# The first lane block of a convolution and feed-forward kernel: x copied in parts, the halo and the second block's loads moved back, the lane's first step ahead of conv(2)'s casts

## The chip, the cores and the metric

One NeuronCore of a Trainium2 chip. Its engines run programs of their own and wait for each other through semaphores: TensorE (PE, matmuls), VectorE (DVE), ScalarE (ACT), GpSimd (POOL) and SyncE (SP, which here only issues DMAs). The metric is the device time of one execution in microseconds, the median of several. Shorter is better.

## The reference

`x` has 8 sequences of 4096 tokens of 192 features. A causal convolution over 7 tokens, with one softmax-normalised filter for each of 8 heads of 24 features, is followed by a gated feed-forward layer:

```python
w = softmax(weight)                                  # 8 heads x 7 taps
out = np.einsum('hk,bskhg->bshg', w, x_unf)          # x_unf: the 7 tokens up to s, zeros before the start
x = out.reshape(B * S, D)                            # 32768 x 192
gate = np.maximum(x @ w_gate, 0.0)                   # 192 x 1536
val = x @ w_val
return (gate * val @ w_out).astype(np.float32)       # 1536 x 192
```

Inputs and outputs are float32; the kernel computes in float16 with float32 sums.

## The kernel before

**Units.** The 32768 tokens go through in 16 units of 1024 token positions, for two sequences ("streams") side by side, one stream on partitions 0 to 63 and one on 64 to 127. Line 692 loops over them. A unit is: the hidden layer for its two windows of 512 (`gate_val`, line 569: per group of 128 hidden features a gate and a value matmul, a relu on ScalarE at line 600, a product on VectorE at line 601), then the output projection in six passes (`project_turn`, line 604: three column groups `p`, each once with window 0 first and once with window 1), then VectorE's `turn_out` (line 626), which transposes a finished group into the output tile, and the stores. Between the first and the second pass over a column group ScalarE does a tiny copy out of that group's PSUM (`between_turns`, line 623). PSUM is a ring of four tiles that all of these share, so a late reader holds up TensorE.

**Two ways to convolve.** The tokens of unit 0 and the first window of unit 1 are convolved by TensorE with band matrices: `conv_steps`, and `conv(2)` (line 402) for the third window. `conv(2)` does eight matmuls, five casts from PSUM on ScalarE (line 426) and five transposing DMAs on SyncE (line 445) into `dense[1]`, which unit 1 reads first. All later windows are convolved by "the lane", one block of two windows for each unit, while TensorE works on something else:

- `lane_load(b)`, line 245: GpSimd issues one load of x for each stream (line 254), cast to float16, into `x_e`, which has one buffer. Block 0 alone also loads a "halo", the 16 tokens ahead of it, into `head` (line 264).
- `lane_turn(b)`, line 455: GpSimd copies `x_e` to `x_p` in another order (line 474, one copy for each stream), and SyncE issues eight DMAs that transpose `x_p` into `x_r` (line 477), which has tokens along the free dimension. The halo is copied from the block before (line 460), or, for block 0, is copied out of `head` (line 464) and transposed by a DMA of its own (line 465).
- `lane_first(b)`, line 527: ScalarE multiplies its part of `x_r` by the first tap into `acc` (line 531, two instructions).
- `lane_rest(b)`, line 538: VectorE adds the other taps (line 542) in 13 steps, dealt out between the `turn_out`s.
- `product(b, k)`, line 503: ScalarE makes products for the rest of the columns (line 506, thirteen instructions, dealt out behind the `between_turns`), which GpSimd adds up (`add`, line 513).

**Order.** The program is scheduled by hand: each engine executes its instructions in the order in which the kernel writes them, and waits where an input isn't there or a buffer isn't free. In the start-up GpSimd issues the loads of the weights, of x and of block 0 in a written order, the output weights' load last (line 689, into the tile `prod0`). At unit 0 come `lane_turn(0)`, `lane_load(1)`, two copies that bring the output weights into `Wo` (line 698), the hidden layer, `conv(2)`, and `lane_first(0)`. SyncE's queue holds, from 10 to 52 us, the issues of the taps (line 353), the halo's transpose, the eight of block 0 and the five of `conv(2)`.

Of the kernel before, what the change touches and what calls it, by code (L numbers as in the profile page):

```python
# [9 lines left out]
F16 = mybir.dt.float16  # L10
# [5 lines left out]
def kernel(  # L16
# [12 lines left out]
    nc = tc.nc  # L29
# [7 lines left out]
    NCH = D // 64  # L37
    NBLK = D // 32
    NFF = DFF // 128
    WIN = 512  # L40
# [12 lines left out]
    HALO = 16  # L53
# [3 lines left out]
    TILES = UNIT // 128  # L57
# [6 lines left out]
    epool = ctx.enter_context(tc.tile_pool(name="epool", bufs=1))  # L64
# [99 lines left out]
    with nc.allow_low_precision("one of the terms is not zero"):  # L164
        nc.vector.tensor_reduce(
            out=Z[:, 112 : 112 + HR],
            in_=eye[:].rearrange("p (g i) -> p i g", i=HR),
# [4 lines left out]
        out=mask[:, :, 0],  # L172
# [69 lines left out]
    def windows(b):  # L242
        return [k for k in (2 * b + 3, 2 * b + 4) if k < 2 * NUNIT]

    def lane_load(b, streams=range(2)):


        n = 4 * len(windows(b))
        if b not in xes:
            xes[b] = epool.tile([128, TILES, 2, NCH, 64], F16, name="x_e"), None  # L250
        xe, head = xes[b]
        for st in streams:
            row = NB * st * S + WIN * (2 * b + 3)
            nc.gpsimd.dma_start(  # L254
                out=xe[:, 0:n, st, :, :].rearrange("p j c r -> p j (c r)"),
                in_=bass.AP(
                    tensor=x.tensor,
                    offset=x.offset + row * D,
                    ap=[[D, 128], [128 * D, n], [1, D]],
                ),  # L260
            )
        if 1 in streams and b == 0:
            head = const.tile([HALO, 2, NCH, 64], F16, name="head")
            nc.gpsimd.dma_start(
                out=head[:].rearrange("p s c r -> p s (c r)"),
                in_=bass.AP(
                    tensor=x.tensor,
                    offset=x.offset + (WIN * 3 - HALO) * D,
                    ap=[[D, HALO], [NB * S * D, 2], [1, D]],
                ),  # L270
            )
        xes[b] = xe, head
# [177 lines left out]
    def second_start(b):  # L450


        return HALO + WIN + HALO * (WIN * (2 * b + 4) % S == 0)

    def lane_turn(b):
        xe, head = xes.pop(b)
        xr = rpool.tile([128, NCH, 2 * (HALO + WIN)], F16, name="x_r")
        if head is None:
            end = second_start(b - 1) + WIN
            nc.gpsimd.tensor_copy(out=xr[:, :, 0:HALO], in_=xrs[b - 1][:, :, end - HALO : end])  # L460
        else:
            turned = const.tile([HALO, NCH, 2, 64], F16, name="turned")
            for st in range(2):
                nc.gpsimd.tensor_copy(out=turned[:, :, st, :], in_=head[:, st, :, :])
            nc.sync.dma_start_transpose(
                out=xr[:, :, 0:HALO], in_=turned[:].rearrange("p c s r -> p (c s r)")
            )
        at = second_start(b)
        if at > HALO + WIN:
            nc.gpsimd.memset(xr[:, :, at - HALO : at], 0.0)  # L470
        n = 4 * len(windows(b))
        xp = epool.tile([128, TILES, NCH, 2, 64], F16, name="x_p")
        for st in range(2):
            nc.gpsimd.tensor_copy(out=xp[:, 0:n, :, st, :], in_=xe[:, 0:n, st, :, :])  # L474
        for j in range(n):
            to = HALO + 128 * j if j < 4 else at + 128 * (j - 4)
            nc.sync.dma_start_transpose(  # L477
                out=xr[:, :, to : to + 128],
                in_=xp[:, j].rearrange("p c s r -> p (c s r)"),
            )  # L480
        xrs[b] = xr

# [55 lines left out]
    def lane_rest(b):  # L538
        acc = accs.pop(b)
        for k in range(1, KW):  # L540
            for at, c, t, n in MINE:
                nc.vector.scalar_tensor_tensor(  # L542
                    out=result(b, at, n) if k == KW - 1 else both(acc, b, at, n),
                    in0=shifted(b, c, k, t, n),
                    scalar=tap[:, c, k : k + 1],
                    in1=both(acc, b, at, n),
                    op0=ALU.mult,
                    op1=ALU.add,
                )
                yield  # L550
        at, c, t, n = POOLS[0]
        nc.vector.tensor_scalar(  # L552
            out=both(prods[b, 0], b, at, n),
            in0=shifted(b, c, 0, t, n),
            scalar1=tap[:, c, 0:1],
            scalar2=None,
            op0=ALU.mult,
        )
        yield
# [9 lines left out]
    def gate_val(u, w):  # L569
        h = hpool.tile([128, NFF, 2, WIN], F16, name="hT")  # L570
        xcb, wb = window(u, w)
        for f in range(NFF):
            if u == 0 and w == 0 and f == CONV1:
                for c in range(NCH):
                    ps = psum.tile([128, 2, 512], FP, name="ps")
                    conv_steps(1, ps, c, range(GSUB))
                    evict(nc.scalar.copy, 1, ps, c)
                passed = psum.tile([128, 2, 512], FP, name="ps")
                nc.vector.memset(passed[:, 0, 0:1], 0.0)
            pss = [psum.tile([128, 2, 512], FP, name="ps") for _ in range(2)]  # L580
            order = [(i, c) for i in range(2) for c in range(NCH)]
            if u == 0 and w == 0 and f == 0:
                order.sort(key=lambda ic: ic[1])
            M = 64 if u else 128
            for i, c in order:
                W = (Wg, Wv)[i]
                for q in range(0, 128, M):
                    for st in range(2):
                        nc.tensor.matmul(  # L589
                            out=pss[i][q : q + M, st, :],  # L590
                            lhsT=W[64 * st : 64 * st + 64, c, 128 * f + q : 128 * f + q + M],
                            rhs=xcb[64 * st : 64 * st + 64, wb, c, :],
                            start=(c == 0),
                            stop=(c == NCH - 1),
                            tile_position=(64 * st, q),
                            skip_group_check=True,
                        )
            for sts in [slice(0, 1), slice(1, 2)] if u == 0 and w == 0 and f == 0 else [slice(0, 2)]:
                gr = gpool.tile([128, 2, WIN], F16, name="gr")
                nc.scalar.activation(out=gr[:, sts], in_=pss[0][:, sts], func=ACTF.Relu)  # L600
                nc.vector.tensor_tensor(out=h[:, f, sts], in0=gr[:, sts], in1=pss[1][:, sts], op=ALU.mult)  # L601
        return h
# [89 lines left out]
    for u in range(NUNIT):  # L692
        if u == 0:
            lane_turn(0)
            lane_load(1)
            wide = plain.rearrange("k (f a p d) -> k f a p d", a=2, p=3, d=32)
            for a in range(2):
                nc.gpsimd.tensor_copy(out=Wo[:, :, :, 32 * a : 32 * a + 32], in_=wide[:, :, a, :, :])
        hs = [gate_val(u, w) for w in range(2)]
        if u == 0:  # L700
            dense[1] = xcpool.tile([128, 2, NCH, WIN], F16, name="xc")
            conv(2)
        bp, w0 = u * UNIT // S, u * UNIT % S // WIN
        lane = None
        if u < NBLOCK:
            lane_first(u)
            lane = lane_rest(u)
        o = opool.tile([128, UNIT // 64, D], FP, name="out_s")
        if u == NUNIT - 1:
            for i in range(4):  # L710
                project(bp, w0 + i // 2, hs[i // 2], i % 2, (4, 2, 1, 1)[i], i == 3, o[:, 4 * i : 4 * i + 4, :])
            continue
        tiles = [None] * 3
        for p, turn in ((0, 0), (1, 0), (0, 1), (2, 0), (1, 1), (2, 1)):
            if turn == 0:
                tiles[p] = psum.tile([128, 2, 512], FP, name="ps")
            project_turn(hs, p, tiles[p], turn)
            if turn == 0:
                between_turns(tiles[p])
                if lane:  # L720
                    for k in TAPS[p]:
                        product(u, k)
                continue
            if lane:
                for _ in range(STEPS[p]):
                    next(lane)
            turn_out(tiles[p], o, p)
        store(o, bp, w0)
        if lane:
            add(u, 0)  # L730
        if u + 1 < NBLOCK:
            lane_turn(u + 1)
        if len(windows(u)) > 1:
            add(u, 1)
        if u + 2 < NBLOCK:
            lane_load(u + 2)
# [30 lines left out]
```

## Time and profile before

| | us |
|---|---|
| median of 3 runs | 762.03 (761.94 to 762.22) |
| the profiled execution, whole | 762.57 |
| span of the profiled execution | 760.9 |
| TensorE busy in the span | 756.1 |
| VectorE, ScalarE, GpSimd busy | 675.3, 610.9, 455.2 |

The profile records one execution. Times in its views are microseconds from the start of the span. A row of a time line gives start, duration, engine, line, operation, output and inputs, shape and count, and in square brackets the idle time of the engine ahead of it with what ended it; neighbouring instructions of one kind are merged in one row. "SPq", "POOLq" and the like are the issuing of a DMA or a wait on the engine's own queue. In the DMA views, q0 is the queue of GpSimd's DMAs, q1 that of SyncE's, q8 the fetching of instructions; their columns are packets, megabytes, and the packets' time as a share of 16 DMA engines; the last number of an issue's row is the time from issue to landing. L12 is line 12 of the kernel.

### The profile page before, as it was taken

The page shows a single profiled execution, that of the slowest core. Times are in us where ns is not written, and L with a number is a line of the kernel's source. Part 1 is how long each engine was busy: PE and PEld are TensorE (multiplying, and loading weights), DVE is VectorE, ACT ScalarE, POOL GpSimd, SP SyncE. Part 2 cuts the span into 40 slices and gives each one's busy share as a digit, 9 for nine tenths or more (in the row PEclk, how much of TensorE's full clock was granted, in tenths as well). Part 3 has the DMA queues.
Part 4 walks back from the last instruction along what each step waited for, and adds up shares of the span by engine and source line. Part 5 has one row for each costly group of instructions (what it writes and reads, how often), then busy time and mean ns, then how long its engine had stood idle before and what let it go on. Part 6 is the DMA issues. An engine that isn't in the chain of part 4 may idle for free.

```text
span 760.9 us, 30515 instructions
## 1 busy us (share of the span) xinstructions
PE 756.1 (99%) x13724; PEld 498.7 (66%) x13724; DVE 675.3 (89%) x647; ACT 610.9 (80%) x681; POOL 455.2 (60%) x297
## 2 busy tenths in 40 slices
PE   9999999999999999999999999999999999999998
PEld 5566666666666666666666666666666666666668
DVE  7879989998998989989899899998999989997891
ACT  7888887888888788887887878788797887877671
POOL 8608649195591946929378392874919659193600
PEclk9999999999999999999999999999999999999999
DMA  9944532345323444244444334452244532140402
GB/s 148 155 54 85 85 73 57 44 90 80 85 44 47 102 67 85 50 59 88 62 85 68 58 78 55 85 85 61 63 49 91 79 80 50 23 100 8 85 2 84
DMA packets 154146, 54.23 MB, mean 71 GB/s; under 512 B 149264, under 2 KB 154016, under 8 KB 154016
## 3 DMA queue, kind: packets, MB, share of 16 engines
q1 hardware_dynamic: 117488, 37.83, 24.3%
q0 software_dynamic: 36096, 14.16, 16.5%
q8 instruction: 107, 1.75, 1.0%
q10 hardware_dynamic: 432, 0.30, 0.1%
q14 instruction: 23, 0.19, 0.1%
HBM read 29.21 MB, written 25.17 MB: 71 GB/s over the span
## 4 chain that ended last, share of the span: by engine, by line
PE 92%; POOL 3%; DVE 2%; SPq 1%; DMA 1%; issue 1%; ACT 0%; ACTq 0%; DVEq 0%; POOLq 0%
PE ps L589 61%; PE ps L611 29%; PE ps L654 2%; SPq L477 1%; DVE acc L542 1%; DMA Wv<-in_moe_w_val_dram 1%; DMA x_r<-x_p 1%; POOL Wv L234 0%; DVE out_s L629 0%; POOL x_p L474 0%; POOL Wg L234 0%; POOL out_s L95 0%; POOL Wg L227 0%; POOL x_e L254 0%; POOL Wv L227 0%
## 5 line engine op out<-in xcount | busy, mean ns | idle before, releaser
L601 DVE TENSOR_TENSOR hT<-gr,ps 128x1024 f16<-128x1024 f16 (+1 forms) x385 | 468.7, 1218 | 35.6 <-ACT gr L600 8.4
L600 ACT ACTIVATE gr<-ps 128x1024 f16<-128x1024 f32 (+1 forms) x385 | 393.0, 1022 | 113.4 <-PE ps L589 113.4
L518 POOL TENSOR_TENSOR prod<-prod,prod 128x896 f32<-128x896 f32 x145 | 303.1, 2090 | 260.6 <-DVE prod L552 226.7
L589 PE MATMUL ps<-xc,Wv 64*64 64x512 f16 (+1 forms) x4464 | 324.5, 376 | 0.7 <-DVE out_s L629 0.7
L589 PE MATMUL ps<-xc,Wg 64*64 64x512 f16 (+1 forms) x4464 | 324.4, 376 | 0.0
L611 PE MATMUL ps<-hT,Wo 64*64 64x512 f16 x4320 | 236.1, 376 | 0.0
L589 PEld LDWEIGHTS <-Wg 64*64 64x64 f16 (+1 forms) x4464 | 164.2, 107 | 84.5 <-POOL Wg L234 0.2
L589 PEld LDWEIGHTS <-Wv 64*64 64x64 f16 (+1 forms) x4464 | 157.3, 106 | 92.1 <-issue 1.3
L611 PEld LDWEIGHTS <-Wo 64*64 64x64 f16 x4320 | 155.2, 107 | 77.8 <-issue 0.3
L506 ACT ACTIVATE prod<-x_r,tap 128x1024 f32<-128x1024 f16 (+2 forms) x195 | 182.7, 1018 | 0.0
L542 DVE SCALAR_TENSOR_TENSOR acc<-x_r,tap,acc 128x1024 f32<-128x1024 f16 (+3 forms) x150 | 118.0, 852 | 4.0 <-ACT acc L531 4.0
L629 DVE STREAM_TRANSPOSE out_s<-ps 128x1024 f32<-128x1024 f32 x45 | 56.1, 1247 | 25.8 <-PE ps L611 24.4
L518 POOL TENSOR_TENSOR xc<-prod,prod 128x896 f16<-128x896 f32 x29 | 60.6, 2090 | 2.3
L474 POOL COPY x_p<-x_e 128x1536 f16<-128x1536 f16 (+1 forms) x30 | 42.0, 1430 | 0.0
L254 POOL DMA_DIRECT2D x_e<-in_x_dram x30 | 26.5, 889 | 0.3 <-POOL x_p L474 0.3
L542 DVE SCALAR_TENSOR_TENSOR xc<-x_r,tap,acc 128x1024 f16<-128x1024 f16 (+3 forms) x30 | 25.1, 838 | 0.0
L531 ACT ACTIVATE acc<-x_r,tap 128x1024 f32<-128x1024 f16 (+3 forms) x30 | 22.5, 801 | 1.9 <-DMA x_r<-x_p 1.9
L624 ACT COPY turned_by<-ps 128x2 f32<-128x2 f32 x45 | 6.9, 154 | 16.3 <-PE ps L611 14.5
L654 PEld LDWEIGHTS <-hT 128*128 128x128 f16 x192 | 15.8, 98 | 0.4 <-issue 0.4
L654 PE MATMUL ps<-Wo,hT 128*128 128x192 f16 x192 | 16.0, 246 | 0.0
L665 ACT COPY out_s<-ps 128x768 f32<-128x768 f32 (+2 forms) x5 | 3.2, 640 | 12.7 <-PE ps L654 12.7
L665 DVE COPY out_s<-ps 128x192 f32<-128x192 f32 x1 | 0.4, 356 | 13.3 <-PE ps L654 13.3
(58 smaller groups left out, 68.1 us busy)
## 6 DMA issues: line engine op xcount, KB each, us to landing
out_dram<-out_s SPq DMA_DIRECT2D x123, 192.0 KB
x_e<-in_x_dram POOLq DMA_DIRECT2D x28, 384.0 KB, 6.3
x_r<-x_p SPq DMA_TRANSPOSE x116
prod<-in_moe_w_out_dram POOLq DMA_DIRECT2D x1, 576.0 KB, 8.9
out_s<-in_x_dram POOLq DMA_DIRECT2D x2, 240.0 KB, 6.2
out_dram<-out_s SPq DMA_DIRECT2D x5, 96.0 KB
prod<-in_x_dram SPq DMA_DIRECT2D x2, 192.0 KB
out_s<-in_x_dram POOLq DMA_DIRECT2D x2, 192.0 KB, 6.4
```

Source lines behind the costliest of these rows:

```text
L254: nc.gpsimd.dma_start(out=xe[:, 0:n, st, :, :].rearrange("p j c r -> p j (c r)"), in_=bass.AP(tensor=x.tensor, offset=x.offset + row * D, ...
L474: nc.gpsimd.tensor_copy(out=xp[:, 0:n, :, st, :], in_=xe[:, 0:n, st, :, :])
L506: nc.scalar.activation(out=both(prods[b, k], b, at, n), in_=shifted(b, c, k, t, n), func=ACTF.Copy, scale=tap[:, c, k : k + 1],)
L518: nc.gpsimd.tensor_tensor(out=acc if k < KW - 1 else xcs[b][:, w, :, :].rearrange("p c t -> p (c t)")[:, LDVE : NCH * WIN], in0=acc, in1=p ...
L531: nc.scalar.activation(out=both(accs[b], b, at, n), in_=shifted(b, c, 0, t, n), func=ACTF.Copy, scale=tap[:, c, 0:1],)
L542: nc.vector.scalar_tensor_tensor(out=result(b, at, n) if k == KW - 1 else both(acc, b, at, n), in0=shifted(b, c, k, t, n), scalar=tap[:, c ...
L589: nc.tensor.matmul(out=pss[i][q : q + M, st, :], lhsT=W[64 * st : 64 * st + 64, c, 128 * f + q : 128 * f + q + M], rhs=xcb[64 * st : 64 * ...
L600: nc.scalar.activation(out=gr[:, sts], in_=pss[0][:, sts], func=ACTF.Relu)
L601: nc.vector.tensor_tensor(out=h[:, f, sts], in0=gr[:, sts], in1=pss[1][:, sts], op=ALU.mult)
L611: nc.tensor.matmul(out=ps[64 * st : 64 * st + 64, b, :], lhsT=Wo[64 * r : 64 * r + 64, f, p, :], rhs=hs[b][64 * r : 64 * r + 64, f, st, :] ...
L629: nc.vector.transpose(out=o[:].rearrange("p t (b d) -> p b t d", b=2)[:, :, :, 32 * p : 32 * p + 32], in_=ps[:].rearrange("p b (t c) -> p ...
L654: nc.tensor.matmul(out=ps[:, i // 2, D * (i % 2) : D * (i % 2) + D], lhsT=h[:, f, st, 128 * q : 128 * (q + 1)], rhs=Wo[:, f, :, :].rearran ...
```

## The change

Three things at unit 0, and nothing else:

- In `lane_turn`, block 0's copies to `x_p` are done in halves: for each stream tiles 0 to 3, then tiles 4 to 7, four copies in place of two. The halo's copies and its transposing DMA come behind the block's copies and its eight transposes, on GpSimd and on SyncE. Later blocks have one part, and their halo copy stays ahead.
- `lane_load(1)` is written behind the two copies into `Wo`.
- `conv(2)` is written behind `lane_first(0)`, so that on ScalarE the lane's first step comes ahead of the five casts. The order on TensorE and VectorE is as before.

```diff
         if head is None:
             end = second_start(b - 1) + WIN
             nc.gpsimd.tensor_copy(out=xr[:, :, 0:HALO], in_=xrs[b - 1][:, :, end - HALO : end])
-        else:
+        at = second_start(b)
+        if at > HALO + WIN:
+            nc.gpsimd.memset(xr[:, :, at - HALO : at], 0.0)
+        n = 4 * len(windows(b))
+        xp = epool.tile([128, TILES, NCH, 2, 64], F16, name="x_p")
+        parts = [slice(0, n)] if head is None else [slice(0, n // 2), slice(n // 2, n)]
+        for st in range(2):
+            for js in parts:
+                nc.gpsimd.tensor_copy(out=xp[:, js, :, st, :], in_=xe[:, js, st, :, :])
+        for j in range(n):
+            to = HALO + 128 * j if j < 4 else at + 128 * (j - 4)
+            nc.sync.dma_start_transpose(
+                out=xr[:, :, to : to + 128],
+                in_=xp[:, j].rearrange("p c s r -> p (c s r)"),
+            )
+        if head is not None:
             turned = const.tile([HALO, NCH, 2, 64], F16, name="turned")
             for st in range(2):
                 nc.gpsimd.tensor_copy(out=turned[:, :, st, :], in_=head[:, st, :, :])
             nc.sync.dma_start_transpose(
                 out=xr[:, :, 0:HALO], in_=turned[:].rearrange("p c s r -> p (c s r)")
             )
-        at = second_start(b)
...
-        for st in range(2):
-            nc.gpsimd.tensor_copy(out=xp[:, 0:n, :, st, :], in_=xe[:, 0:n, st, :, :])
...
         if u == 0:
             lane_turn(0)
-            lane_load(1)
             wide = plain.rearrange("k (f a p d) -> k f a p d", a=2, p=3, d=32)
             for a in range(2):
                 nc.gpsimd.tensor_copy(out=Wo[:, :, :, 32 * a : 32 * a + 32], in_=wide[:, :, a, :, :])
+            lane_load(1)
         hs = [gate_val(u, w) for w in range(2)]
         if u == 0:
             dense[1] = xcpool.tile([128, 2, NCH, WIN], F16, name="xc")
-            conv(2)
         bp, w0 = u * UNIT // S, u * UNIT % S // WIN
         lane = None
         if u < NBLOCK:
             lane_first(u)
             lane = lane_rest(u)
+        if u == 0:
+            conv(2)
```

More of the change, by code (lines that the diff above doesn't have):

```diff
@@ L466, in lane_turn @@
                 out=xr[:, :, 0:HALO], in_=turned[:].rearrange("p c s r -> p (c s r)")
-            )
-        at = second_start(b)
[L469 to L472, printed above, removed]
-        for st in range(2):
[L474 to L479, printed above, removed]
             )
```

## The prediction

> **What bounds the kernel now.** I read the page's first lines, then TensorE's waits, then the time lines of TensorE, ScalarE, GpSimd and SyncE between 16 and 62 us, and last the DMA queues stretch by stretch.
>
> ```profile
> span 760.9 us, 30515 instructions
> PE 756.1 (99%) x13724; PEld 498.7 (66%) x13724; DVE 675.3 (89%) x647; ACT 610.9 (80%) x681; POOL 455.2 (60%) x297
> ```
>
> TensorE is busy for 756.1 of 760.9 us. Whatever the change frees on another engine counts only as far as it closes a gap on TensorE, and all gaps together are 4.8 us. Of TensorE's waits for another engine, the only one after the kernel's first 10 us lies where the change works:
>
> ```profile
> PE ps L589 <- DVE out_s L629: 0.7, 1, 0.7
> ```
>
> TensorE's time line shows it:
>
> ```profile
> 41.48 15.80 PE L611 MATMUL ps<-hT,Wo 64*64 64x512 f16 x288
> 57.08 0.84 PE L589 MATMUL ps<-xc,Wg 64*64 64x512 f16 x12
> 57.73 0.85 PE L589 MATMUL ps<-xc,Wv 64*64 64x512 f16 x12
> 58.38 0.84 PE L589 MATMUL ps<-xc,Wg 64*64 64x512 f16 x12
> 59.90 0.84 PE L589 MATMUL ps<-xc,Wv 64*64 64x512 f16 x12 [0.68 <-DVE out_s L629]
> 60.55 0.84 PE L589 MATMUL ps<-xc,Wg 64*64 64x512 f16 x12
> 61.24 0.84 PE L589 MATMUL ps<-xc,Wv 64*64 64x512 f16 x12
> ```
>
> Unit 0's output projection (six passes, 41.48 to 57.08, so 2.60 us each) is followed by unit 1's hidden layer, in groups that start 0.65 us apart (57.73 - 57.08). The sixth group should start at 57.08 + 5 x 0.65 = 60.33 and starts at 61.24. **0.91 us** is lost, and that is all that can be won here. Who loses it is on ScalarE:
>
> ```profile
> 41.14 2.00 ACT L426 CAST out_s<-ps 112x480 f16<-112x480 f32 x5 [0.17 <-PE ps L413]
> 45.08 1.55 ACT L531 ACTIVATE acc<-x_r,tap 128x1024 f32<-128x1024 f16 x2 [1.94 <-DMA x_r<-x_p]
> 46.53 0.14 ACT L624 COPY turned_by<-ps 128x2 f32<-128x2 f32 x1
> ...
> 58.92 1.92 ACT L600 ACTIVATE gr<-ps 128x1024 f16<-128x1024 f32 x2
> ```
>
> ScalarE does conv(2)'s five casts, stands still 1.94 us until the lane's transposed x has landed, does the lane's first step, the little copy of line 624 and thirteen products, and comes to unit 1's first relu at 58.92. VectorE's lane steps hang on the same first step, and its last transpose (58.62) frees the PSUM that the 59.90 group waits for:
>
> ```profile
> 58.62 1.24 DVE L629 STREAM_TRANSPOSE out_s<-ps 128x1024 f32<-128x1024 f32 x1
> ```
>
> So both ways lead back to one moment, the landing of x_r. The chain of waits has it (issue of the last transpose, and the time until it counted as landed):
>
> ```profile
> 40.55 4.21 DMA x_r<-x_p
> ```
>
> I call the moment **T**; it is 44.77 now. The page's execution takes 762.57 us for a span of 760.9; the runs' median is 762.03. I work out differences in the span and put them on the median.
>
> **The change, part by part.** What T costs first. Now the relu starts 13.84 us after the lane's first step (58.92 - 45.08), which starts 0.31 after T. The change puts the casts behind that step: from start to start they take about 1.95 us. The relu then starts at T + 0.31 + 13.84 + 1.95 = T + 16.1. The sixth group starts 2.32 after the relu (61.24 - 58.92), so at T + 18.42, if that is later than 60.33. The loss is T - 41.9 in place of 0.91, and the difference is **T - 42.8**, never under -0.91 (T at 41.9 or before). ScalarE's moved casts are thus no gift: they now fill a hole of 1.94 us, and afterwards they lie behind T. T must come about 2 us earlier for the kernel to stand still.
>
> A second path has the same threshold. The third pass, which adds to the first pass's PSUM, starts at 41.48 + 2 x 2.60 = 46.68 and has to come after the copy of line 624, which reads that PSUM (now done at 46.67). Afterwards that copy ends at T + 0.31 + 1.45 + 1.95 + 0.14 = T + 3.85: in time for T up to 42.8, and from there TensorE waits for it, 1 us for each us of T. Two other users of T have room. VectorE's last transpose ends 15.1 after T and is needed at 59.03, so T up to 43.9. Conv(2)'s transposes:
>
> ```profile
> 26.82 1.22 SPq L465 DMA_TRANSPOSE x_r<-turned  x1
> 29.64 12.17 SPq L477 DMA_TRANSPOSE x_r<-x_p  x8
> 43.16 7.62 SPq L445 DMA_TRANSPOSE xc<-out_s  x5
> ```
>
> ```profile
> 45.69 2.55 SPq L445 DMA_TRANSPOSE xc<-out_s  x2
> ```
>
> ```profile
> 49.36 1.42 SPq L445 DMA_TRANSPOSE xc<-out_s  x1
> ```
>
> The fourth of them is issued at 45.69 + 2.55/2 = 46.97; the fifth overlaps it in the target, waits for its landing and is issued at 49.36. So an undisturbed transpose lands **2.4 us** after its issue starts. The five take 49.36 + 2.4 - 43.16 = 8.6 us from the end of the casts, which will be T + 3.7; TensorE reads the result at 57.08: T up to 44.8.
>
> Now T itself. GpSimd's order around it:
>
> ```profile
> 19.15 0.87 POOL L254 DMA_DIRECT2D x_e<-in_x_dram  x1
> ...
> 23.18 1.03 POOL L689 DMA_DIRECT2D prod<-in_moe_w_out_dram  x1
> 26.17 0.62 POOL L464 COPY turned<-head 16x192 f16<-16x192 f16 x2 [1.96 <-DMA head<-in_x_dram]
> 26.75 2.87 POOL L474 COPY x_p<-x_e 128x1536 f16<-128x1536 f16 x2
> 29.91 1.75 POOL L254 DMA_DIRECT2D x_e<-in_x_dram  x2 [0.30 <-POOL x_p L474]
> 32.16 2.24 POOL L698 COPY Wo<-prod 128x1152 f16<-128x1152 f16 x2 [0.50 <-DMA prod<-in_moe_w_out_dram]
> 59.11 10.75 POOL L518 TENSOR_TENSOR prod<-prod,prod 128x896 f32<-128x896 f32 x5 [24.71 <-ACT prod L506]
> ```
>
> ```profile
> x_e<-in_x_dram POOLq DMA_DIRECT2D x1, 384.0 KB, 6.8
> ```
>
> ```profile
> L474 POOL COPY x_p<-x_e x30: 830/1472/1482, 26.7 to 678.3; 128x1536 f16<-128x1536 f16 x28, 128x768 f16<-128x768 f16 x2
> ```
>
> Today GpSimd stands 1.96 us for the halo rows, copies both streams whole, and the first big transpose starts at 29.64. A half copy (128x768) is 0.83 us in the last lane block. Afterwards the two halves of stream 0 run from 24.21 to 25.9, beside what was a wait; stream 1 lands at 19.15 + 6.8 = 25.95, its first half is copied by 26.8, its second by 27.6, the halo rows by 28.2. Four halves cost 3.3 us for 2.87, hidden, since Wo's copies wait for their DMA until 32.1 anyway. SyncE's tap issues lie ahead of line 465, which started at 26.82, so its queue is free by then. The first transpose can start at **26.8, 2.8 us earlier**. The eight take 12.17 us, the halo's 1.22 now comes behind them: the queue is done at 40.2 (41.8 now). If nothing else held it, the halo's would start at 39.0 and land 2.4 later, T = 41.4: the full 0.91 won.
>
> But something else holds it. The DMA queues between 32.3 and 35 us, in the middle of the 12.17 us in which the eight are issued:
>
> ```profile
> q0 software_dynamic: 1170, 0.44, 143.0%
> q1 hardware_dynamic: 2, 0.00, 0.1%
> ```
>
> q0 is GpSimd's queue (here the second block's two loads), q1 SyncE's. While a load runs, the transposes get 2 packets of 1172. Afterwards Wo's copies go first, 32.16 to 34.40 as now, and the loads are issued at 34.4 to 36.2 in place of 29.9 to 31.7. Nobody waits for them before the next block's copies, which stand behind the sums that begin at 59.11, and Wo's copies, needed at 41.48, lose nothing. The loads move 4.5 us later, from the middle of the transposes to their **end**: the seven earlier ones get through before, the eighth (issued at about 37.7) and the halo's (39.0) meet them. The loads' times to landing, second block's second load of now and the pair of the next block, when no transposes were about:
>
> ```profile
> x_e<-in_x_dram POOLq DMA_DIRECT2D x1, 384.0 KB, 8.0
> ```
>
> ```profile
> x_e<-in_x_dram POOLq DMA_DIRECT2D x2, 384.0 KB, 5.8
> ```
>
> The second load, issued at 35.3, lands between 41.1 (5.8) and 43.3 (8.0). The tail has two transposes to move then; the bounds are nothing and 1 us. T lies between 41.4 and 44.3. I take 42.5 for the load, nearer the 8.0 because two transposes are in its way as seven are now, and 0.5 for the tail: **T = 43.0**, a difference of +0.2.
>
> T itself has an accident in it today. In the stretch from 42 to 44 us (40 slices of 0.05 us):
>
> ```profile
> GB/s 184 210 246 184 225 215 123 67 10 1 1 328 0 0 0 0 0 0 0 0 0 0 0 0 0 0 0 0 0 0 0 0 0 0 0 0 0 0 0 0
> ...
> q8 instruction: 1, 0.02, 3.1%
> ```
>
> The last transpose's data are through at 42.45; then one engine takes a packet of instructions (the 328 at 42.55), and the landing counts at 44.77, 2.3 us after the data, where the fourth transpose above needed 2.4 us for issue, data and all. About 1.6 us of T is that packet (estimate: 2.3 less the 0.7 or so that are left of those 2.4 behind 1.3 of issue and the data). It can miss the new tail or hit it again; I take it as missed, with 0 and +1.6 as bounds.
>
> **A rule of the Trainium skill on this.** "DMA: Bandwidth & Descriptors", section "Queues, rings and completion order", says that each DMA engine goes round between the queues that have work, one packet of some 9 to 17 descriptors at a time. By that the tail would share the engines with the load rather than wait for it, and T would be near 41.4. The 2 packets against 1170 above speak against so fine a turn, so it is a rival and not the forecast.
>
> All later blocks keep one part, and the halo copy stays ahead of it, so nothing changes behind unit 0. GpSimd's next work (59.11) waits for ScalarE's products, and moves with T as TensorE does.
>
> **The rivals.**
> 1. *Full gain.* The tail gets its turn between the loads' packets: T = 39.0 + 2.4 = 41.4, below 41.9, so -0.91: **761.1 us**. For it: SyncE is done 1.6 us earlier even with nine transposes, and the instruction packet may miss. Against: the 1170 to 2.
> 2. *Slower.* The lane's first step stands at the head of ScalarE's queue, and behind it wait the casts, the copy of line 624 and all products, thus TensorE's third pass from 46.68 on. Decides from T = 42.8; at T = 44.3 (second load at 43.3 and the whole 1 us of tail) it costs 1.5, with an instruction packet in the tail (T up to 45) 2.2: **763.2 to 764.2 us**. For it: the q8 row above, and two loads moved onto the tail. Against: the loads get through faster when fewer transposes disturb them (5.8).
> 3. *It doesn't split.* The first transpose waits for all four part copies: start at 27.6, not 26.8, and the halo's at 39.8. As the load ends at 42.5 anyway, T and the time stay as forecast; no case of its own.
>
> **How the numbers follow.** Forecast: T = 43.0, +0.2 us in the span, 762.03 + 0.2 = **762.2 us**, chance 0.58 for T from 42.0 to 44.1 (761.2 to 763.3). Full gain 0.20, slower 0.22. 0.2%, 1.52 us, is about what a measurement of this kernel can tell from no change: faster than 760.5 is not in reach, since the gap is 0.91, so 0.02 for what I overlook; slower than 763.55 needs T above 44.3, half of the second rival, 0.11; the rest, 0.87, is within. The range from 760.9 to 763.8 holds the full gain with 0.2 for the measurement and leaves out the upper part of the second rival, where the tail and the packet both come late.
>
> **What would show it.** Right: the first transpose of the lane at about 26.8 and the last, the halo's, at 38 to 39; the loads' issue at 34.4; between 37 and 41 us q1 with next to no packets beside a full q0; the lane's first step at T + 0.3 with ScalarE idle for 1.5 to 2.5 us before it and the casts right behind it; TensorE's third pass at 46.7 to 47. Wrong: a first transpose that starts at 27.5 or later, or is issued but runs only after 32, when the output weights have landed (they fill q0 until then; if it holds up the whole row and not only the first, T moves out to 44 and the second rival holds); a halo that lands before 42 (the first rival); a sixth group that starts earlier than T + 18.4 after T above 43, which would say that ScalarE's order isn't the binding one.

## The result, and the profile after

The changed kernel takes 764.59 us (median of 14 runs, 763.09 to 765.6), the kernel before 762.21 us on the same chip (14 runs, 761.52 to 763.66). The ratio is 1.0028, 95% interval 1.002 to 1.0036: **slower by 2.1 us**, 1.5 to 2.7 (by the ratio; the medians differ by 2.4), where 762.2 us was forecast with a range up to 763.8. The profiled execution took 764.22 us, with a span of 762.5.

Page and TensorE's waits of the changed kernel:

```profile
span 762.5 us, 30519 instructions
PE 757.0 (99%) x13724; PEld 498.4 (65%) x13724; DVE 675.6 (89%) x647; ACT 610.2 (80%) x681; POOL 455.1 (60%) x299
```

```profile
PE ps L613 <- ACT turned_by L626: 0.9, 1, 0.9
PE ps L196 <- PEq L754: 0.8, 1, 0.8
PE ps L591 <- DVE hT L603: 0.4, 1, 0.4
```

The wait of before is gone (0.7 us for VectorE's transpose), and two others have come in its place: TensorE's third projection pass waits for the little copy out of PSUM, and the sixth group of unit 1 for a product that stands behind a late relu. (The wait at L196 lies in the kernel's first microsecond and is there before as well, with 0.8 us.) Lines behind 460 have moved by two: L613, L626, L591, L602, L508, L533 are the L611, L624, L589, L600, L506, L531 of before. TensorE's time line, with the two gaps in the rows that start at 48.34 and 62.84:

```profile
42.09 5.37 PE L613 MATMUL ps<-hT,Wo 64*64 64x512 f16 x96
48.34 10.55 PE L613 MATMUL ps<-hT,Wo 64*64 64x512 f16 x192 [0.88 <-ACT turned_by L626]
...
62.84 0.84 PE L591 MATMUL ps<-xc,Wv 64*64 64x512 f16 x12 [0.41 <-DVE hT L603]
```

ScalarE, from its last relu of unit 0 on:

```profile
40.55 1.02 ACT L602 ACTIVATE gr<-ps 128x1024 f16<-128x1024 f32 x1 [0.27 <-PE ps L591]
44.80 1.55 ACT L533 ACTIVATE acc<-x_r,tap 128x1024 f32<-128x1024 f16 x2 [3.23 <-DMA x_r<-turned]
46.26 1.97 ACT L426 CAST out_s<-ps 112x480 f16<-112x480 f32 x5
48.10 0.20 ACT L626 COPY turned_by<-ps 128x2 f32<-128x2 f32 x1
```

It stands still for 3.23 us at the lane's first step with the casts ready behind it. The landing T was to come about 2 us earlier to pay for that, and it has hardly moved: 44.49 in place of 44.77. The chain of waits names it, and what follows from it:

```profile
37.96 6.53 DMA x_r<-turned
```

GpSimd and SyncE did what was planned, to a few tenths of a microsecond: four half copies from 24.17, the loads at 34.06, the first transpose at 26.65. The halo's is issued at 37.96, 1 us ahead of the 39.0 of the sum.

```profile
24.17 3.23 POOL L469 COPY x_p<-x_e 128x768 f16<-128x768 f16 x4
27.34 0.63 POOL L479 COPY turned<-head 16x192 f16<-16x192 f16 x2
31.88 2.23 POOL L699 COPY Wo<-prod 128x1152 f16<-128x1152 f16 x2 [3.92 <-DMA prod<-in_moe_w_out_dram]
34.06 1.75 POOL L254 DMA_DIRECT2D x_e<-in_x_dram  x2
```

```profile
26.65 11.21 SPq L472 DMA_TRANSPOSE x_r<-x_p  x8
37.96 1.17 SPq L480 DMA_TRANSPOSE x_r<-turned  x1
```

So the first and the last transpose were issued 3.0 and 2.6 us earlier, and the last landed hardly earlier. The DMA queues from 31 to 33 us, from 37 to 39 and from 39.5 to 42 (packets, megabytes, share):

```profile
q1 hardware_dynamic: 1162, 0.27, 110.3%
q8 instruction: 1, 0.02, 3.7%
q0 software_dynamic: 13, 0.00, 1.7%
```

```profile
q0 software_dynamic: 920, 0.35, 149.2%
q1 hardware_dynamic: 30, 0.00, 2.1%
```

```profile
q0 software_dynamic: 612, 0.23, 111.0%
q1 hardware_dynamic: 455, 0.11, 46.7%
```

First the transposes have the engines to themselves; then the first of the two loads leaves them 30 packets in 950; then the second load and the transposes share, and both are slow. The median of the two loads' times to landing is 7.6 us, and the first alone has 5.9, so the second took 2 x 7.6 - 5.9 = 9.3 us (9.4 unrounded, from 34.93 to 44.3):

```profile
x_e<-in_x_dram POOLq DMA_DIRECT2D x2, 384.0 KB, 7.6
```

```profile
x_e<-in_x_dram POOLq DMA_DIRECT2D x1, 384.0 KB, 5.9
```

### The profile page after: what moved, and what is told of

The parts are those of the page before. It is cut to its first block, busy times and chain, and to the rows that moved or that the text cites. A ratio compares the mean times of both kernels' runs of the same rounds, so it can differ in the third digit from the quotient of the medians.

```text
span 762.5 us, 30519 instructions
## 1 busy us (share of the span) xinstructions
PE 757.0 (99%) x13724; PEld 498.4 (65%) x13724; DVE 675.6 (89%) x647; ACT 610.2 (80%) x681; POOL 455.1 (60%) x299
## 4 chain that ended last, share of the span: by engine, by line
PE 92%; POOL 2%; DMA 2%; ACT 1%; SPq 1%; DVE 1%; issue 0%; ACTq 0%; POOLq 0%
PE ps L591 61%; PE ps L613 29%; PE ps L656 2%; SPq L472 1%; DMA Wv<-in_moe_w_val_dram 1%; DMA x_r<-turned 1%; ACT prod L508 1%; POOL x_p L469 0%; POOL Wg L227 0%; POOL Wv L227 0%; POOL Wv L234 0%; ACT out_s L426 0%; POOL x_e L254 0%; DVE acc L544 0%; ACT acc L533 0%
## 5 line engine op out<-in xcount | busy, mean ns | idle before, releaser
L602 ACT ACTIVATE gr<-ps 128x1024 f16<-128x1024 f32 (+1 forms) x385 | 392.7, 1021 | 113.9 <-PE ps L591 113.8
L591 PE MATMUL ps<-xc,Wv 64*64 64x512 f16 (+1 forms) x4464 | 324.2, 376 | 0.4 <-DVE hT L603 0.4
L591 PE MATMUL ps<-xc,Wg 64*64 64x512 f16 (+1 forms) x4464 | 324.2, 376 | 0.1
L613 PE MATMUL ps<-hT,Wo 64*64 64x512 f16 x4320 | 236.3, 376 | 0.9 <-ACT turned_by L626 0.9
L591 PEld LDWEIGHTS <-Wg 64*64 64x64 f16 (+1 forms) x4464 | 163.6, 107 | 85.2 <-issue 0.4
L591 PEld LDWEIGHTS <-Wv 64*64 64x64 f16 (+1 forms) x4464 | 157.0, 106 | 92.1 <-issue 0.9
L613 PEld LDWEIGHTS <-Wo 64*64 64x64 f16 x4320 | 155.3, 107 | 78.8 <-issue 1.3
L508 ACT ACTIVATE prod<-x_r,tap 128x1024 f32<-128x1024 f16 (+2 forms) x195 | 182.7, 1020 | 0.0
L533 ACT ACTIVATE acc<-x_r,tap 128x1024 f32<-128x1024 f16 (+3 forms) x30 | 22.5, 801 | 3.2 <-DMA x_r<-turned 3.2
L626 ACT COPY turned_by<-ps 128x2 f32<-128x2 f32 x45 | 7.0, 157 | 16.3 <-PE ps L613 14.5
```

The costliest lines, as they stand in the source:

```text
L508: nc.scalar.activation(out=both(prods[b, k], b, at, n), in_=shifted(b, c, k, t, n), func=ACTF.Copy, scale=tap[:, c, k : k + 1],)
L533: nc.scalar.activation(out=both(accs[b], b, at, n), in_=shifted(b, c, 0, t, n), func=ACTF.Copy, scale=tap[:, c, 0:1],)
L591: nc.tensor.matmul(out=pss[i][q : q + M, st, :], lhsT=W[64 * st : 64 * st + 64, c, 128 * f + q : 128 * f + q + M], rhs=xcb[64 * st : 64 * ...
L613: nc.tensor.matmul(out=ps[64 * st : 64 * st + 64, b, :], lhsT=Wo[64 * r : 64 * r + 64, f, p, :], rhs=hs[b][64 * r : 64 * r + 64, f, st, :] ...
```

## The experiments

Twelve runs were made, ten of other kernels and one more profile each of the kernels before and after, in three batches, each beside the kernel before on its own chip. Theory A is the one that the prediction's slower rival already had: the lane's first step at the head of ScalarE's queue makes everything behind it wait for T, and the loads, moved onto the transposes' tail, keep T late. Rivals: the moved loads cost the time whatever ScalarE's order (B); the gap of 0.91 us is what the kernel before usually has (C); the split or the halo at the end makes the loss. The changed kernel's three parts are called the split, the loads and the order.

**The order alone** (`p3_first_ahead`, on the kernel before):

```diff
-            conv(2)
         bp, w0 = u * UNIT // S, u * UNIT % S // WIN
...
             lane = lane_rest(u)
+        if u == 0:
+            conv(2)
```

> The kernel before with one part of the change: the lane's first step ahead of conv(2)'s casts on ScalarE, nothing else. T is the landing of block 0's transposed x, 44.8 in the kernel before, 44.5 in the changed one. Theory A (ScalarE's order decides: the time differs by T - 42.8): T stays 44.8, so +2.0 us, ScalarE idle for about 3.8 us ahead of the lane's first step, and TensorE waits about 2 us for the copy out of PSUM behind the first two passes. Rival B (the loads moved onto the transposes cost the time, the order on ScalarE is harmless): within 0.3 us of before.

Measured: 762.11 us against 762.07, ratio 1.0006 (0.9997 to 1.0014). Neither 2.0 us slower nor a proof of B, for T was not 44.8: in its profile the lane's first step starts at 42.65.

```profile
42.65 1.55 ACT L531 ACTIVATE acc<-x_r,tap 128x1024 f32<-128x1024 f16 x2 [1.30 <-DMA x_r<-x_p]
44.11 1.98 ACT L426 CAST out_s<-ps 112x480 f16<-112x480 f32 x5
45.95 0.20 ACT L624 COPY turned_by<-ps 128x2 f32<-128x2 f32 x1
```

The copy ends at 46.15, in time for the third pass, and nothing is lost. Ahead of T this kernel does what the kernel before does, so T itself must vary from one execution to the next, and the kernel before needs a second look.

**The kernel before, again** (`before_again`, unchanged):

> The kernel before, unchanged, for another profile. Theory A (refined): the profile on which the prediction rests caught a late landing, T = 44.8, because a packet of instructions stood ahead of the last transpose on one DMA engine; usually T is 42 to 43.2, the casts are done at 43.1 anyway, and TensorE has next to no gap at unit 1 (0 to 0.3 us where 0.91 was lost). Rival C (the landing at 44.8 is usual): T = 44.8 and 0.9 us lost again.

Measured: 762.24 us in one run, span 760.5. C falls: the lane's first step starts at 43.64, as the last cast ends (43.78), without any wait, and TensorE has no gap at unit 1: its sixth group starts 60.92 - 57.68 = 3.24 us after the first, five groups of 0.65. ScalarE's rows, then TensorE's:

```profile
41.78 2.00 ACT L426 CAST out_s<-ps 112x480 f16<-112x480 f32 x5 [0.17 <-PE ps L413]
43.64 1.59 ACT L531 ACTIVATE acc<-x_r,tap 128x1024 f32<-128x1024 f16 x2
```

```profile
57.68 0.82 PE L589 MATMUL ps<-xc,Wg 64*64 64x512 f16 x12
...
60.92 0.82 PE L589 MATMUL ps<-xc,Wv 64*64 64x512 f16 x12
```

In the stretch from 42 to 44 us the packet of instructions is there again, but only after the transposes' data:

```profile
GB/s 143 169 251 195 241 215 215 205 148 67 36 10 1 1 1 0 0 0 0 0 0 0 328 0 0 0 0 0 0 0 0 0 0 0 0 0 0 0 0 0
```

The data end at 42.6, the packet comes at 43.1. In the first profile the two met at 42.55. The traces have sixteen steps of a semaphore for each of these transposes, and T is the last of them. In the first profile fifteen come between 42.78 and 42.93 and the last at 44.77; in the second all sixteen lie between 42.93 and 43.08, so T is 43.1 there. The gap of 0.91 us was an accident of that one execution, and the packet of instructions is its likely cause.

**Without the order** (`p1p2_casts_first`: split and loads, casts first as before):

```diff
         if u == 0:
             dense[1] = xcpool.tile([128, 2, NCH, WIN], F16, name="xc")
+            conv(2)
...
-        if u == 0:
-            conv(2)
```

> The changed kernel with conv(2)'s casts back ahead of the lane's first step. Theory A: T stays 44.5, but now only T - 44.8 counts, so -0.3 us against the kernel before (-0.6 to +0.3), 1.9 us less than the changed kernel. Rival B: as slow as the changed kernel, +1.6 to +2.1 us.

Measured: 762.68 us against 762.07, ratio 1.0012 (1.0003 to 1.0021). B expected 1.6 to 2.1 us over the kernel before; it is 0.9, with 0.2 to 1.6 as the interval. Below the changed kernel it is by 1.2 us (by the ratios) to 1.9 us (by the medians, 764.59 there, on another chip), where A had 1.9. A's own number, -0.3, was too low: by the rule at the end of this section, T = 44.5 gives 762.3, so about 0.5 comes from measuring from the accidental gap, and the rest would be a T that is later in the median. In the profile the first step starts at 46.09:

```profile
46.09 1.55 ACT L533 ACTIVATE acc<-x_r,tap 128x1024 f32<-128x1024 f16 x2 [1.87 <-DMA x_r<-turned]
```

**Without the loads** (`p1p3_loads_early`: split and order, `lane_load(1)` where it was):

```diff
             lane_turn(0)
+            lane_load(1)
...
-            lane_load(1)
```

> The changed kernel with the second block's loads back ahead of the output weights' copies, so that they are issued at about 28 us, behind block 0's and the halo's copies. The loads then follow the output weights in GpSimd's DMA queue with no pause, and the transposes wait for the end of both, about 36.5, and drain in 0.4 to 0.9 us each: T 42 to 44. Theory A: T - 42.8, so -0.6 to +1.2, likeliest +0.3 us. Rival B: the loads are off the tail, so no slower than before, -0.9 to 0.

Measured: 762.19 us against 762.07, ratio 1.0008 (0.9998 to 1.0017). The first step starts at 41.71, so T is 41.4, a little earlier than the 42 to 44 that was expected.

```profile
41.71 1.55 ACT L533 ACTIVATE acc<-x_r,tap 128x1024 f32<-128x1024 f16 x2 [0.53 <-DMA x_r<-turned]
```

By the ratios, the split with the loads costs 0.9 us and the split with the order 0.6, the order by itself 0.5; loads and order together cost 2.1.

**The loads held back** (`hold_loads`, on the changed kernel):

```diff
+            gate = const.tile([128, 1], F16, name="gate")
+            nc.gpsimd.tensor_copy(out=gate[:], in_=xrs[0][:, 0, 0 : 0 + 1])
             lane_load(1)
```

> The changed kernel with the second block's loads held until the halo's transpose has landed: GpSimd copies one column of it into a spare tile ahead of lane_load(1). No load runs beside the transposes after the output weights. Theory A: T = 38.0 + 2.4 = 40.4, ScalarE goes from its last relu to the lane's first step without a stop, and the whole gap of 0.91 us on TensorE is closed: 0.9 us faster than before, 2.5 to 3.0 faster than the changed kernel. A rival that puts the loss on ScalarE's order alone, whatever T is, or on something outside this place, expects it to stay at +1.6 or more.

Measured: 761.88 us against 762.07, ratio 1.0001 (0.9992 to 1.001). The rival that blames the order whatever T is falls: the order is unchanged and the loss is gone. The halo has landed at 39.7, when GpSimd's wait for it ends, and ScalarE doesn't stop. GpSimd's rows, then ScalarE's:

```profile
39.78 0.19 POOL L701 COPY gate<-x_r 128x1 f16<-128x1 f16 x1 [5.44 <-DMA x_r<-turned]
40.02 1.75 POOL L254 DMA_DIRECT2D x_e<-in_x_dram  x2
```

```profile
40.86 1.54 ACT L533 ACTIVATE acc<-x_r,tap 128x1024 f32<-128x1024 f16 x2
```

The 0.9 us that it was to win over the kernel before aren't there, since that kernel usually has nothing to win: here the profile has no gap, and the kernel isn't measurably faster.

**Held back, casts first** (`hold_casts_first`: the same with `conv(2)` ahead of the lane's first step):

> The changed kernel with the loads held until the halo's transpose has landed, and conv(2)'s casts ahead of the lane's first step as before. Theory A: T about 40, both orders on ScalarE then cost the same, no gap at unit 1: as fast as the held kernel with the lane first, 0 to 0.5 us faster than before, whose gap is usually closed too. If ScalarE's order cost anything by itself, this one would be faster than the held kernel with the lane first by 0.5 us or more.

Measured: 762.27 us against 762.2, ratio 0.9999 (0.999 to 1.0008). With T early the two orders cost the same. The two held kernels are no faster than the kernel before by anything that can be measured, so no better version follows from this.

**Without the split** (`p2p3_no_split`: loads and order, whole copies and the halo first):

> The changed kernel without the first part: whole copies of block 0's x, the halo's transpose first, but the second block's loads behind the output weights' copies and the lane's first step ahead of the casts. The transposes then start at about 29.3, so four or five of them meet the loads in place of three. Theory A: T 44.5 to 45.5, so +2.0 to +3.5 us against the kernel before, as slow as the changed kernel or slower. A rival by which the split itself, or the halo at the end, makes the loss expects it within 0.5 us of before.

Measured: 764.48 us against 762.16, ratio 1.0031 (1.002 to 1.0042). As slow as the changed kernel: the split doesn't make the loss, and it doesn't lessen it either. More transposes meet the loads, and T is 44.58:

```profile
44.90 1.55 ACT L531 ACTIVATE acc<-x_r,tap 128x1024 f32<-128x1024 f16 x2 [3.07 <-DMA x_r<-x_p]
```

**The split alone** (`p1_split_only`):

> The kernel before with the first part alone: four part copies and the halo last, the loads and ScalarE's order as before. Theory A: T 41 to 42.5 as with the loads early and the lane first, and the casts ahead as before, so nothing is lost and little can be won: -0.4 to +0.2 us. The rival by which the split or the halo at the end makes the loss: +1.5 to +2.1.

Measured: 762.16 us against 762.16, ratio 0.9997 (0.9988 to 1.0006): nothing lost, nothing won. Its profile is of the slowest of its runs (763.93 us), with a first step as late as 46.43, where T was expected at 41 to 42.5:

```profile
46.43 1.55 ACT L533 ACTIVATE acc<-x_r,tap 128x1024 f32<-128x1024 f16 x2 [3.17 <-DMA xc<-out_s]
```

The view names a transpose of `conv(2)`; by the halo's own semaphore T is 46.1, again 0.31 ahead of the step. The loads were issued at 27.71 here and at 27.78 in the run without the loads, where T is 41.4. Between 40 and 42.5 us GpSimd's queue still moved 76 packets here and none there. So early loads don't make T early in every execution; that they do so as a rule is read from the medians.

**A third load** (`more_loads`, on the changed kernel):

```diff
             lane_load(1)
+            again = epool.tile([128, TILES, D], F16, name="again")
+            nc.gpsimd.dma_start(
+                out=again[:],
+                in_=bass.AP(
+                    tensor=x.tensor,
+                    offset=x.offset + WIN * 5 * D,
+                    ap=[[D, 128], [128 * D, TILES], [1, D]],
+                ),
+            )
```

> The changed kernel with a third load of the same size behind the second block's two, into a tile that nothing reads. Theory A (the transposes' tail waits for GpSimd's loads): T moves out by one load more, 1.5 to 2.5 us, to about 46.5, and the time by as much: +3.6 to +4.6 us against the kernel before. A rival by which ScalarE's order or the order on SyncE alone makes the loss: the same as the changed kernel, +1.6 to +2.4.

Measured: 764.53 us (5 runs) against 762.16, ratio 1.0035 (1.0023 to 1.0047), so 1.8 to 3.6 us slower than the kernel before, about as slow as the changed kernel. The expectation, 3.6 to 4.6 with T at 46.5, was wrong: the tail doesn't wait until GpSimd's queue is empty. The third load, issued at 35.54, takes 10.4 us, to 45.9, and the lane's first step stands at 45.09 already.

```profile
x_e<-in_x_dram POOLq DMA_DIRECT2D x1, 384.0 KB, 9.2
again<-in_x_dram POOLq DMA_DIRECT2D x1, 384.0 KB, 10.4
```

```profile
45.09 1.55 ACT L533 ACTIVATE acc<-x_r,tap 128x1024 f32<-128x1024 f16 x2 [3.78 <-DMA x_r<-turned]
```

So the transposes are served between and beside the loads, as in the third stretch above. The rival that blames ScalarE's order expected no change from a third load, and this run doesn't exclude it; the held loads do.

**The loads in four and in eight pieces** (`loads_in_4`, `loads_in_8`, on the changed kernel; same bytes, with 2 or 4 in place of `k`):

```diff
-            lane_load(1)
+            xes[1] = epool.tile([128, TILES, 2, NCH, 64], F16, name="x_e"), None
+            for st in range(2):
+                for j in range(0, TILES, TILES // k):
+                    nc.gpsimd.dma_start(
+                        out=xes[1][0][:, j : j + TILES // k, st, :, :].rearrange("p j c r -> p j (c r)"),
+                        in_=bass.AP(
+                            tensor=x.tensor,
+                            offset=x.offset + (NB * st * S + WIN * 5 + 128 * j) * D,
+                            ap=[[D, 128], [128 * D, TILES // k], [1, D]],
+                        ),
+                    )
```

> The changed kernel with the second block's two loads cut into four of half the size, same bytes, same place in GpSimd's order. Theory A1 (a DMA engine works off one of GpSimd's loads before it turns to a transpose): the stretch in which the transposes stand still halves from about 2.7 to 1.4 us and they get more turns, so T 43.0 to 44.0 in place of 44.5 and the time 0.5 to 1.5 us under the changed kernel. Theory A2 (the load queue goes first until it is empty, or the two share by bytes): T and the time as in the changed kernel, +1.6 to +2.4 us against before.

> The same with eight loads of a quarter. GpSimd then issues for about 7 us. Theory A1: next to no stretch without transposes, T 41 to 42.5, so -0.2 to +0.7 us against the kernel before. Theory A2: T as in the changed kernel, or later by what the longer issue puts off, +1.6 us or more.

Measured: four pieces 764.2 us against 762.2, ratio 1.0025 (1.0016 to 1.0034); eight pieces 763.55, ratio 1.0016 (1.0007 to 1.0025). By the medians that is 0.4 and 1.0 us under the changed kernel's 764.59: in A1's direction, but less than A1 asked for, and the intervals overlap the changed kernel's. Their profiles can't decide it, since one is of the fastest of its runs and the other of the slowest (762.51 and 764.96 us); ScalarE's row with four pieces, then with eight:

```profile
43.12 1.55 ACT L533 ACTIVATE acc<-x_r,tap 128x1024 f32<-128x1024 f16 x2 [2.09 <-DMA x_r<-turned]
```

```profile
45.55 1.55 ACT L533 ACTIVATE acc<-x_r,tap 128x1024 f32<-128x1024 f16 x2 [3.67 <-DMA x_r<-turned]
```

By what rule the two queues share stays open.

**The changed kernel, again** (`after_again`):

> The changed kernel, unchanged, for another profile. Theory A: T between 44 and 45 again (44.5 in the first profile), the copy out of PSUM at about 48 and TensorE's third pass behind it, the sixth group of unit 1 at T + 18.4. If T were 43 or less here, the first profile was not typical and the loss has another source.

Measured: 764.21 us in one run, span 762.5. The first step starts at 44.80, as in the first profile to the hundredth, after 2.93 us without work.

```profile
44.80 1.55 ACT L533 ACTIVATE acc<-x_r,tap 128x1024 f32<-128x1024 f16 x2 [2.93 <-DMA x_r<-turned]
```

T is 44.5 again, but the two queues share otherwise. From 38.5 to 39 us, with the first load still under way (to 39.45), the transposes move 270 packets to the loads' 136; from 39.5 to 40.5, with the second load alone, they get next to nothing:

```profile
q0 software_dynamic: 488, 0.19, 155.0%
q1 hardware_dynamic: 47, 0.00, 7.4%
```

**All profiles on one line.** Each profile gives two starts, that of the lane's first step on ScalarE and that of unit 0's projection on TensorE, and its execution's own time:

| kernel | order | first step | projection | own time | own time less first step | less projection |
|---|---|---|---|---|---|---|
| changed | lane first | 44.80 | 42.09 | 764.22 | **719.42** | 722.13 |
| changed, again | lane first | 44.80 | 42.38 | 764.21 | **719.41** | 721.83 |
| without the split | lane first | 44.90 | 42.33 | 764.42 | **719.52** | 722.09 |
| a third load | lane first | 45.09 | 41.82 | 764.53 | **719.44** | 722.71 |
| loads in 4 | lane first | 43.12 | 41.54 | 762.51 | **719.39** | 720.97 |
| loads in 8 | lane first | 45.55 | 42.39 | 764.96 | **719.41** | 722.57 |
| order alone | lane first | 42.65 | 41.86 | 762.06 | **719.41** | 720.20 |
| without the loads | lane first | 41.71 | 41.69 | 761.82 | 720.11 | **720.13** |
| loads held | lane first | 40.86 | 41.48 | 761.62 | 720.76 | **720.14** |
| before | casts first | 45.08 | 41.48 | 762.57 | **717.49** | 721.09 |
| without the order | casts first | 46.09 | 42.56 | 763.65 | **717.56** | 721.09 |
| split alone | casts first | 46.43 | 41.60 | 763.93 | **717.50** | 722.33 |
| before, again | casts first | 43.64 | 42.12 | 762.24 | 718.60 | **720.12** |
| loads held, casts first | casts first | 43.65 | 42.13 | 762.27 | 718.62 | **720.14** |

One rule gives all fourteen within 0.1 us: the time is the later of *projection + 720.13* (TensorE without a gap) and *first step + 719.42* with the lane first, or *first step + 717.50* with the casts first. The two orders differ by 1.92 us, the casts. By the same rule the changed kernel's median, 764.59, means a first step at 45.2 (T = 44.9). With the casts first a step at 45.2 gives 762.7, the median measured without the order.

## Why the prediction was wrong, point by point

The mechanism was right: it is the second rival, "slower", with the copy of line 624 as the door through which ScalarE's lateness reaches TensorE. So were the starts on GpSimd and SyncE, the split (the first transpose did not wait for all four copies), the cost of the moved casts (1.95 us foretold, 1.92 by the table), and the sum: the sixth group was to start at T + 18.42 and starts at 62.84 - 44.49 = T + 18.35.

Two terms failed.

*"T = 43.0, a difference of +0.2."* T is 44.5 in both profiles of the changed kernel, and 44.9 by the median: 1.5 to 1.9 us later. It was put together from the second load's landing (42.5, so 7.2 us after an issue at 35.3) and a tail of 0.5. The tail was sized right, 0.2 and 0.5 us in the two profiles. The load was not: it landed at 44.3 and 43.9, with 9.4 and 9.1 us from issue, above the upper end of 8.0 that was taken from the kernel before. Load and transposes slow each other: in the next block of the kernel before, with no transposes about, the second of the two loads takes 2 x 5.8 - 5.3 = 6.3 us, and with the loads held the halo's transpose takes 2.3 us (37.43 to 39.73) in place of 6.53. The sharing that the first rival asked for is there in some stretches (455 packets to 612), but it didn't make T early.

On the rule of the Trainium skill ("DMA: Bandwidth & Descriptors", "Queues, rings and completion order"), that a DMA engine goes round between its queues packet by packet, the traces are divided: the stretch with 455 packets to 612 agrees, those with 30 to 920 and 47 to 488 don't, although transposes had been issued and hadn't landed (whether their packets were ready on the engines, the traces don't say).

The packet of instructions, which the prediction took as missed with +1.6 as the bound, did miss: the halo's sixteen semaphore steps lie between 44.20 and 44.49 in one profile and between 44.17 and 44.48 in the other.

*"I work out differences in the span and put them on the median."* The profile of before had T = 44.77 and lost 0.91 us; the median run loses nothing. The prediction saw the accident ("T itself has an accident in it today") and named its 1.6 us, but used it only for the changed kernel's range and not for the point from which the difference was counted. Own time and median, 762.57 and 762.03, already hinted at it: 0.5 us, more than the 0.28 between the runs. By the rule of the table, T = 43.0 would have given 719.42 + 43.31 = 762.7 and not 762.2.

The two make up the miss: 762.2 + 0.5 + 1.9 = 764.6. This closes by construction, since T = 44.9 was worked back from the median; with the 44.5 of the profiles it gives 764.2, the own time of both. The slower rival was priced at 763.2 to 764.2 with 0.22, and with T up to 45 (its costs of 1.5 and 2.2 us give 763.5 to 764.2); the price lacked the same 0.5. The first rival (full gain) could not happen on the median, since the gain was not there: the two kernels that do close the gap, with the loads held, stand at 761.88 and 762.27.

## What to carry to other kernels

An engine's queue is in order: before a step that waits for a DMA is put ahead of work that is ready, ask what the ready work covers now, for moved behind the wait it is paid in full (1.92 us here), and it stays free only as long as the data come early in every run. A load that nobody waits for isn't harmless where it runs beside a transfer that somebody does wait for; issue it once that transfer has landed, when its own slack allows. And before a gap in one profile is taken as what can be won, compare that execution's own time with the median: where it is longer, the gap may belong to that execution alone.

## What the runs showed of the hardware

- A load of 384 KB that GpSimd issued, the second of a pair, took 9.4 and 9.1 us to land beside transposes from SyncE's queue, and 6.3 us in the next block with none about. How the two queues share changes within an execution and from one to the next: transposes to loads, 30 packets to 920 and 455 to 612 in one profile of the changed kernel, 270 to 136 and 47 to 488 in the other.
- In one profile the last of a transpose's sixteen semaphore steps came 1.84 us after the fifteenth (44.77 and 42.93), with a packet of instructions on one DMA engine at 42.55. That the packet put it off is likely but not shown: no run tried it by itself. The prediction had worked it out at about 1.6 us. In a second profile of the same kernel the packet came half a microsecond after the data and cost nothing.
- The start of unit 0's projection, ahead of which the change does nothing to TensorE, varies between 41.48 and 42.56 us over the fourteen profiles. With ScalarE early this goes into the time one to one (720.12 to 720.14 behind it in four profiles), with ScalarE late not at all.
